# A long convolution and a state-space layer on one core: spectra kept on one partition, output stage in array pieces, queues in a new order

## The chip, the cores and the metric

The kernel runs on one core of a Trainium2 chip. A core has a matrix engine (TensorE, PE in the profile, with PEld for its weight loads), a vector engine (VectorE, DVE), a scalar engine (ScalarE, ACT), GpSimd (POOL) and SyncE (SP); POOL and SP issue nearly all transfers here, and sixteen DMA engines carry them. Each engine works through its own instructions in order. The metric is device time in microseconds; lower is better.

## The reference, cut to what matters

Two layers with S = 2048 positions and D = 1024 channels in bfloat16; their results stand side by side in the output, 2048 x 2048.

```python
# A: short causal convolution, gate, long convolution by FFT, gate
k_shift = sum over t < 4 of k_pad[:, t:t+S, :] * shift_k[:, 3 - t]
kv = k_shift * v
y  = irfft(rfft(kv, 2*S) * rfft(ssm_k, 2*S))[:S]      # along the positions
a  = q * (y + kv * ssm_D)
# B: diagonal complex state space
Bu = x @ B_bar.T                                      # complex, P = 1024 states
h  = Lam_bar * h + Bu[t]        for every position t
b  = 2 * real(hseq @ C.T) + x * Dskip
out = concatenate([a, b])
```

Lam_bar and B_bar come from the small parameters Lambda, log_dt and B.

## The kernel before, in words

All work is cut into some 1240 tasks. Each task is a small function stored under a short name in the table `E`; a hand-written string `ORDER` (lines 66 to 144) lists the tasks one after another. A word such as `sa.1.0:d0` calls `E["sa"](1, 0)` and gives it PSUM buffer `d0`. The letters behind the colon are buffers: `p` single and `d` double accumulator banks in PSUM (two `p`, three `d`), `a`, `b`, `e`, `m`, `w` rings of tiles in SBUF. A suffix `@S` or `@G` puts a transfer on SP's or POOL's queue, `@D` or `@G` puts a copy on the vector engine or GpSimd. Since every engine takes its instructions in program order, the string fixes the order on all of them. Line 168 (`spd`) and line 169 (`gpd`) issue the transfers: SP unless the word says G, POOL unless it says S.

Layer A is a Fourier transform of length 4096 at odd half frequencies, split as 128 x 32, with 16 residues r of the position.

- `kp`, `vp` load k and v; `kvm`, `kva`, `kvb`, `kvc` (lines 575 to 604) form the gated product on the vector engine, two residues at a time, eight chains in all. `am` (610) multiplies by the first-stage matrix `F1t`, `ae` evicts, `ast` stores to the scratch tensor `Ys_kv` in DRAM.
- `hl` loads the filter, `hT` (630) transposes it on PE, `hm` (643) transforms it, `he` evicts, `hst` stores to `Ys_h`.
- The second stage runs over 16 groups gq of frequencies. `lh` and `lk` load a group's 512 KB from the two scratch tensors, `lw` a pair of groups' weights. `sh` and `sk` (668 to 681) transform it with 64x64 pieces of the array, four matmuls a call; `she` and `ske` evict. Real and imaginary part of a spectrum then stand in different blocks of 32 partitions. For the complex product the other part is needed too: `sw` (694) copies each block of 32 partitions of `hab` to its neighbour with four DMAs a group. `pr` (701) multiplies on the vector engine, `sa` (707) does the first half of the inverse with eight 64x64 matmuls a call and two calls a group, `sae` evicts, `vst` stores to `Vs`.
- The output stage: `vl` loads a residue from `Vs`, `a3` (739) multiplies by `Gt`, 128 x 128, half of which is zeros; `a3e` evicts, `qm` multiplies by q (loaded by `qp`), `ost` stores.

Layer B runs over 16 chunks i of 128 positions. `bl`, `bT`, `bc` load, transpose and copy the 16 blocks of B to `BT`; `cx` and `x` (480, 483) bring C and x through transposing DMAs on SP. `U` (486) is the input product, 16 matmuls of 128 columns a call; `ue` evicts; `r1`, `r2`, `sc`, `cm`, `r3`, `r4` (500 to 537) are rotation, scan, carry and rotation back on the vector engine, one chunk after another; `y` (539) is the output product, four matmuls of 512 columns a call, `ye` evicts and `yst` stores. The order string mixes layer B's U and y blocks between the steps of layer A.

The parameters, their tables (`tabA1`, `par_rest`, `eo`, `stt`) and the broadcast of the short filter (`ld_w`, `wb`, `wbe`) stand in the first lines of the string. Tiles of the pool a1 (the ring of k and the broadcast filter) give way to those of a2 once the first stage is done.

Of the kernel before, what the change touches and what calls it, by code (L numbers as in the profile page):

```python
# [27 lines left out]
def a_constants():  # L28
# [4 lines left out]
    G1 = np.zeros((2, 2, 32, 2, 64, 2))  # L33
    for h in range(2):
        F1[:, h, :, h] = np.transpose(F, (0, 2, 1, 3))
        G1[h, :, :, :, :, h] = np.transpose(F, (1, 3, 2, 0)) * (2 / NFFT)
# [5 lines left out]
    WF = np.zeros((2, N2, 2, 32, 3, N2))  # L42
# [3 lines left out]
    WF[:, :, :, :, 2, :] = WF[:, :, :, :, 0, :]  # L46
    WI = np.zeros((2, 2, N2, 16, 2, 2, N2, 2))
    for gi in range(2):
        for ui in range(2):
            for gq in range(16):  # L50
                cc = np.transpose(c_[ui, 2 * gq + gi], (1, 0)); ss = np.transpose(s_[ui, 2 * gq + gi], (1, 0))
                o = WI[gi, :, :, gq, ui]
                o[0, :, 0, :, 0] = cc; o[0, :, 0, :, 1] = ss
                o[1, :, 0, :, 0] = -cc; o[1, :, 0, :, 1] = -ss
                for cp in range(2):
                    o[cp, :, 1, :, 0] = -ss; o[cp, :, 1, :, 1] = cc
    W = np.concatenate([WF.reshape(128, NWP, 4 * 96), WI.reshape(128, NWP, 2 * 256)], axis=2)
# [9 lines left out]
ld_par bl.4.0@G:b0 bl.5.0@G:b1 bl.5.1@G:b2 bl.4.1:b3 bl.6.0:b4 bl.2.1@G:b5 ld_sd@S bl.1.1@G:b6 ld_w@S:a0a1 kp.0@G kp.-2 ld_F par_T:p0 hl.2@G:a2  # L67
bl.7.0:b7 bT.4.0:p1 p32 exp1 bl.6.1:b8 hl.3@G:a3 bc.4.0 dve2 x.0:b9 kp.-1@G bT.5.0:p0 dve3 sm_pre bT.4.1:p1 bc.5.0 hl.1@G:a4 bl.0.1:b10 bc.4.1
bl.7.1@G:b11 x.4:b12 bT.6.0:p0 tabA1:a5a6a7a8 bc.6.0 bl.2.0:b13 hl.0:a9 exp2 bl.0.0:b0 sin0 rt@G kp.1 bT.1.1:p1 x.2:b1 bT.5.1:p0 tabA2 bc.1.1 cx.4.1
wb.7:p1 bc.5.1 par_rest vp.0@G:a10 ld_G@S sin2 wb.4:p0 cx.5.1 wbe.4 sin1 wb.6:p0 cx.0.0 wbe.6@D eo.0 bl.3.1:b3 wb.1:p0 wbe.7@D bl.1.0:b4 wbe.1@D  # L70
wb.2:p1 cx.0.1 eo.1 stt.0 wb.0:p0 cx.7.0 wbe.2 stt.1 eo.3 wb.5:p1 bl.3.0:b6 x.1:b2 wbe.5@D wbe.0 stt.3 wb.3:p1 wbe.3 bT.6.1:p0 cx.1.0 dd bT.2.0:p1
# [75 lines left out]
def full_kernel(ctx, tc, A_q, A_k, A_v, A_shift_k, A_ssm_k, A_ssm_D, B_x, B_Lre, B_Lim, B_Bre, B_Bim,  # L147
# [96 lines left out]
    def k8(name, shape):  # L244
        return rtile(ap_pool("a2"), "e", name, shape)
# [3 lines left out]
    def once(key, make):  # L249
        if key not in st:  # L250
            st[key] = make()
        return st[key]
# [571 lines left out]
```

## Time and profile before

| | us |
|---|---|
| median of 3 runs | 378.71 |
| lowest and highest run | 377.25, 380.74 |
| span of the profiled execution | 378.5 |
| PE busy in it | 346.6 |
| DVE busy in it | 324.6 |
| ACT busy in it | 264.2 |
| POOL busy in it | 81.3 |

The span goes from the first to the last instruction of the profiled execution, which has no other time of its own. A line of the profile names the source line (L492), the engine, the operation, and the tiles as output <- inputs. Busy time is a union over instructions; a matmul's recorded length includes its way through the array, so the spacing of starts says more than the mean length. The sixteen DMA engines moved 100.06 MB, 264 GB/s on average; the SP queue's packets took 54.8% and POOL's 36.8% of their time.

### The profile page before, as it was taken

To read this page: it belongs to the slowest core of one execution; us is meant where nothing else is said; L and a number is where in the kernel's file an instruction comes from. 1 tells how busy PE (TensorE), PEld (TensorE's weight loads), DVE (VectorE), ACT (ScalarE), POOL (GpSimd) and SP (SyncE) were. 2 spreads that over 40 slices of the span, in tenths; PEclk is the share of its full clock that TensorE was granted. 3 is DMA by queue.
4 is the path that set the end of the run, shared out by engine and by line. 5 is a ranking of instruction groups with operands and counts; after the bars stand their busy time and mean duration, and the time that the engine had idled before them with its cause. 6 is when DMAs were issued, how large, how long until landed. Compare 5 with 4: busy or idle time off the path is not lost.

```text
span 378.5 us, 8748 instructions
## 1 busy us (share of the span) xinstructions
PE 346.6 (92%) x3661; PEld 225.6 (60%) x3661; DVE 324.6 (86%) x229; ACT 264.2 (70%) x341; POOL 81.3 (21%) x150
## 2 busy tenths in 40 slices
PE   4548889899899999999999999989999999999995
PEld 3226678785455578855444757367867664467442
DVE  6989599999999997999997797576899999993972
ACT  4978798877778886952785879778869771346433
POOL 7300023022112521214200325330210202211021
PEclk9999999999999999999999999999999999999999
DMA  6999999997578999999999897999989539877995
GB/s 231 317 338 216 265 272 286 296 314 235 200 243 270 247 313 287 281 272 268 190 275 312 258 324 234 220 267 221 284 236 312 175 125 325 306 229 255 350 319 206
DMA packets 67418, 100.06 MB, mean 264 GB/s; under 512 B 38435, under 2 KB 42147, under 8 KB 67380
## 3 DMA queue, kind: packets, MB, share of 16 engines
q1 hardware_dynamic: 54660, 56.32, 54.8%
q0 software_dynamic: 12720, 43.19, 36.8%
q8 instruction: 28, 0.46, 0.5%
q14 instruction: 10, 0.08, 0.1%
HBM read 49.16 MB, written 33.55 MB: 219 GB/s over the span
## 4 chain that ended last, share of the span: by engine, by line
PE 56%; DMA 15%; issue 13%; ACT 7%; SPq 4%; POOL 2%; DVE 1%; POOLq 0%; ACTq 0%; DVEq 0%
PE ps_u L492 22%; PE ps_y L546 16%; PE ps_a L744 4%; DMA wts<-a_c_W 4%; SPq L483 4%; DMA Ys_kv<-ysb 3%; PE ps_a L643 3%; DMA l2k<-Ys_kv 3%; DMA ld<-in_B_B_re_dram 3%; PE ps_a L717 3%; PE ps_a L610 3%; DMA hab<-hab 2%; PE ps_a L676 2%; PE ps_t L630 2%; ACT ysb L615 2%
## 5 line engine op out<-in xcount | busy, mean ns | idle before, releaser
L492 PEld LDWEIGHTS <-BT 128*128 128x128 bf16 x2048 | 119.3, 98 | 22.6 <-issue 11.7
L492 PE MATMUL ps_u<-xT,BT 128*128 128x128 bf16 x2048 | 127.7, 219 | 2.4 <-ACT u L497 1.2
L546 PE MATMUL ps_y<-CT,h 128*128 128x512 bf16 x512 | 127.7, 379 | 0.0
L546 PEld LDWEIGHTS <-h 128*128 128x128 bf16 x512 | 44.6, 98 | 48.0 <-issue 6.1
L523 DVE TENSOR_TENSOR_SCAN h<-rtab,h 128x2080 bf16<-128x2080 f32 x16 | 71.8, 4488 | 0.2
L497 ACT CAST u<-ps_u 128x512 bf16<-128x512 f32 x64 | 38.2, 603 | 27.0 <-PE ps_u L492 19.1
L506 DVE TENSOR_TENSOR mt<-u,Z 128x4096 bf16<-128x4096 bf16 x16 | 36.7, 2291 | 15.8 <-ACT u L497 15.4
L704 DVE TENSOR_TENSOR hab<-x,hab 128x4096 bf16<-128x4096 bf16 x16 | 36.5, 2286 | 15.2 <-DMA hab<-hab 10.5
L556 ACT CAST yo<-ps_y 128x512 bf16<-128x512 f32 x32 | 19.1, 596 | 28.0 <-PE ps_y L546 24.4
L650 ACT CAST ysbh<-ps_a 128x1024 bf16<-128x1024 f32 x32 | 32.3, 1033 | 8.8 <-PE ps_a L643 7.5
L691 ACT CAST x<-ps_a 128x1024 bf16<-128x1024 f32 x32 | 31.9, 1026 | 8.8 <-PE ps_a L676 5.9
L506 DVE TENSOR_TENSOR mt<-h,Z 128x4096 bf16<-128x4096 bf16 x16 | 36.7, 2292 | 0.5
L724 ACT CAST vsb<-ps_a 128x1024 bf16<-128x1024 f32 x32 | 31.7, 1027 | 6.5 <-PE ps_a L717 6.0
L583 DVE TENSOR_TENSOR mt<-kring,wbc 128x2048 bf16<-128x2048 bf16 (+3 forms) x14 | 35.8, 2592 | 0.4 <-ACT wbc L473 0.2
L615 ACT CAST ysb<-ps_a 128x1024 bf16<-128x1024 f32 x32 | 32.3, 1043 | 2.7 <-issue 1.6
L685 ACT CAST hab<-ps_a 128x1024 bf16<-128x1024 f32 x32 | 32.2, 1030 | 2.1 <-PE ps_a L676 1.9
L551 PE MATMUL ps_y<-Dd,xT 128*128 128x128 bf16 x128 | 28.0, 219 | 0.0
L749 ACT CAST ot<-ps_a 128x1024 bf16<-128x1024 f32 x16 | 15.7, 1018 | 14.1 <-PE ps_a L744 14.1
L169 POOL DMA_DIRECT2D Ys_h<-ysbh x20 | 14.3, 716 | 43.3 <-ACT ysbh L650 43.3
L168 POOL DMA_DIRECT2D hab<-hab x32 | 15.6, 494 | 32.1 <-ACT hab L685 18.3
L458 PE MATMUL ps_t<-ident,ld 128*128 128x128 bf16 x128 | 13.9, 285 | 9.1 <-DMA ld<-in_B_B_re_dram 4.4
L643 PE MATMUL ps_a<-hT,F1t 128*128 128x512 bf16 x64 | 20.6, 402 | 0.8 <-ACT ysbh L650 0.6
(116 smaller groups left out, 381.8 us busy)
## 6 DMA issues: line engine op xcount, KB each, us to landing
Ys_h<-ysbh POOLq DMA_DIRECT2D x20, 256.0 KB, 5.5
l2h<-Ys_h SPq DMA_DIRECT2D x9, 512.0 KB, 9.7
Vs<-vsb SPq DMA_DIRECT2D x9, 512.0 KB, 4.3
vv<-Vs SPq DMA_DIRECT2D x9, 512.0 KB, 5.2
Ys_kv<-ysb POOLq DMA_DIRECT2D x17, 256.0 KB, 6.2
l2k<-Ys_kv SPq DMA_DIRECT2D x8, 512.0 KB, 3.9
hab<-hab SPq DMA_DIRECT2D x32, 128.0 KB, 5.4
l2k<-Ys_kv POOLq DMA_DIRECT2D x8, 512.0 KB, 7.8
```

Source lines behind the costliest of these rows:

```text
L492: nc.tensor.matmul(pu[:, w, jl, :], BT[:, 2 * jp + jl, w, d, :], xT[:, d, :], start=(d == 0), stop=(d == ND - 1))
L497: nc.scalar.copy(u[:, :, 2 * jp:2 * jp + 2, :], st["pu", i, jp][:])
L506: nc.vector.tensor_mul(m, s_, w_)
L523: nc.vector.tensor_tensor_scan(gf, rtab[:].rearrange("p a j t -> p (a j t)"), gf, 0.0, ALU.mult, ALU.add)
L546: nc.tensor.matmul(py[:], h[:, 1 - w, j, 2:TP], CT[:, j, w, dh * 512:(dh + 1) * 512], start=(j == 0 and w == 0), stop=(j == NJ - 1 and w = ...
L583: nc.vector.tensor_mul(m[:, :, j0:j0 + n, :], a_, wbc[:, j0:j0 + n, :].unsqueeze(1).to_broadcast([P, 2, n, DV]))
L615: nc.scalar.copy(st["ysb", r, u][:], st["pa", r, u][:].rearrange("p e d -> p (e d)"))
L643: nc.tensor.matmul(pd[:, e, :], F1t[:, u, :], st["hT", f, rp][:, e, :], start=True, stop=not sk)
L650: nc.scalar.copy(st["yh", f, rp, u][:], st["pa", f, rp, u][:])
L685: nc.scalar.copy(hab[:, a, :, e * 512:(e + 1) * 512], st["ps", key, gq, e][:])
L691: nc.scalar.copy(x16[:, :, e * 512:(e + 1) * 512], st["ps", "k", gq, e][:])
L704: nc.vector.tensor_mul(hab, x16.unsqueeze(1).to_broadcast([P, 2, 2 * D]), hab)
```

## The change

The matrices and tasks of the second and third stage of layer A, and the order string as a whole.

- `sh` and `sk` now compute only the real or only the imaginary part of a group in a call (argument `c_`), for both halves of the channels, with eight matmuls of 64 rows and 32 columns of the array. Real and imaginary part of one frequency thus land on the same partition, side by side in the free dimension. The weights lose the repeated block.
- `sw` and its 64 DMAs are gone. `pr` writes all four products of a real or imaginary part with another to a tile of its own: still 4096 elements a partition.
- `sa` is one call a group with 32 matmuls of 32 rows and 64 columns of the array. It sums the four products with three weight blocks (the weights of a group pair grow from 896 to 1024 columns) and takes two double banks at once.
- `vl` loads two residues of one half u. `a3` uses 64x64 pieces without the zeros of the old matrix, eight matmuls a call, two calls for each of eight pairs of residues. `qm` works on a pair at once. `qp` and `ost` move 64 partitions, 256 KB, each.
- The vector engine's working tile (`mt`) moves from the common ring to the pools a1 and a2; `hab`'s pool has two buffers instead of three, and four more `a` buffers come in a2. The raw parameters lie in unused rows of `ones`. `kp` of the shifted start loads three slots in one task instead of four in two.
- The order string is written anew for every engine and queue. Of its start: eleven of the sixteen B loads are on POOL (six before), three transposing loads stand ahead of the first `U` (fourteen before), the filter's transposes and `hm` come earlier, and the broadcast filter's copies are all on ACT, while eight `bc` copies are on the vector engine (two before). Before the output stage it has `vst.14@G vl.0.1@S:a6 r1.13:m0 r2.13 y.11.0.1 y.10.0.2 vl.0.0@S:a0 a3.0.0:d0 a3.0.1:d2`.

```diff
-    def s2(key, nm, gq, e, o):
+    def s2(key, nm, gq, c_):
         wt = st["w", gq // 2]
         pd = dtile("ps_a")
...
+        for e in range(2):
+            for gi in range(2):
+                for u in range(2):
+                    up = slice(64 * u, 64 * u + 64)
+                    x = 32 * (2 * (u ^ gi) + e)
+                    b0 = ((2 * gq + gi) % 4) * 64 + 32 * c_
+                    nc.tensor.matmul(pd[x:x + 32, u, :], wt[up, b0:b0 + 32],
+                                     st[nm, gq][up, gi, e * 512:(e + 1) * 512], start=True, stop=True,
+                                     tile_position=(64 * u, x))
...
+    def s2e(key, nm, gq, c_):
+        t_ = once((nm, gq), lambda: k4(nm, [P, 2, D]))
+        nc.scalar.copy(t_[:, c_, :], st["ps", key, gq, c_][:].rearrange("p e d -> p (e d)"))
...
-    def sw(gq):
-        hab = st["hab", gq]
-        for b in range(4):
-            o = b ^ 1
-            spd(hab[32 * b:32 * b + 32, 1, :, :], hab[32 * o:32 * o + 32, 0, :, :])
...
     def pr(gq):
-        hab = st["hab", gq][:].rearrange("p a u d -> p a (u d)")
-        x16 = st["x16", gq][:].rearrange("p u d -> p (u d)")
-        nc.vector.tensor_mul(hab, x16.unsqueeze(1).to_broadcast([P, 2, 2 * D]), hab)
+        st["m2", gq] = rtile(ap_pool("a2"), "e", "hab", [P, 2, 2, D])
+        nc.vector.tensor_mul(st["m2", gq][:], st["x16", gq][:].unsqueeze(2).to_broadcast([P, 2, 2, D]),
+                             st["h16", gq][:].unsqueeze(1).to_broadcast([P, 2, 2, D]))
...
-    def sa(gq, e):
...
+    def sa(gq):
+        wt, m = st["w", gq // 2], st["m2", gq]
+        pd = [dtile("ps_a") for _ in range(2)]
+        st["ps", "v", gq] = pd
+        for n_, (a, b, wi) in enumerate(((0, 0, 0), (1, 1, 1), (0, 1, 2), (1, 0, 2))):
+            for e in range(2):
+                for s in range(2):
+                    for u in range(2):
+                        x = 32 * (2 * s + e)
+                        b0 = 4 * 64 + (gq % 2) * 384 + (3 * u + wi) * 64
+                        nc.tensor.matmul(pd[s][64 * u:64 * u + 64, e, :], wt[x:x + 32, b0:b0 + 64],
+                                         m[x:x + 32, a, b, u * 512:(u + 1) * 512], start=(n_ == 0), stop=(n_ == 3),
+                                         tile_position=(x, 64 * u))
...
-    def a3_(r):
...
+    def a3_(r, dh):
+        pd = dtile("ps_a")
+        st["po", r, dh] = pd
+        for u in range(2):
+            for e in range(2):
+                for h in range(2):
+                    ep, hp = slice(64 * e, 64 * e + 64), slice(64 * h, 64 * h + 64)
+                    nc.tensor.matmul(pd[hp, e, :], Gt[ep, u, :], st["vv", r, u][ep, h, dh * 512:(dh + 1) * 512],
+                                     start=(u == 0), stop=(u == 1), tile_position=(64 * e, 64 * h))
...
+    E["ost"] = lambda r, h: gpd(oar[h, r], st["ot", r][64 * h:64 * h + 64, :, :])
```

294 lines of the change are left out of this document (134 added, 160 removed).

## The prediction

> **What bounds the kernel now.** I read the page's busy shares and slices first, then the time chain, then busy times by stage, then the groups by line.
>
> ```profile
> span 378.5 us, 8748 instructions
> ...
> PE 346.6 (92%) x3661; PEld 225.6 (60%) x3661; DVE 324.6 (86%) x229; ACT 264.2 (70%) x341; POOL 81.3 (21%) x150
> ...
> PE   4548889899899999999999999989999999999995
> ```
>
> PE (the matrix engine) is at eight tenths or more from the fifth slice to the last but one, so the question is how much of that is dense work. The chain gives the pace where PE itself is the chain; its columns are start, length, what.
>
> ```profile
> 6.99 4.90 SPq L483
> ...
> 12.71 8.41 SPq L483
> 21.17 5.62 DMA ld<-in_B_B_re_dram
> ...
> 44.11 1.05 PE ps_u L492 x16
> ...
> 127.35 0.86 PE ps_y L546 x4
> ...
> 142.52 0.86 PE ps_a L610 x4
> ...
> 204.53 0.89 PE ps_u L492 x16
> ...
> 224.74 0.56 PE ps_a L717 x8
> ...
> 227.16 0.99 PE ps_a L717 x16
> ...
> 361.12 1.73 PE ps_a L744 x8
> ...
> 374.69 0.58 ACT yo L556
> ```
>
> Sixteen 128-column matmuls take 0.89 us (56 ns each), four 512-column ones 0.86 (216 ns). In the 64x64 array pieces eight more matmuls cost 0.99 - 0.56 = 0.43 us, 54 ns each: a quarter of 216, so four pieces do run at once. The output stage (L744) runs full size, 1.73 / 8 = 216 ns.
>
> ```profile
> 0.00:50.00 50.00, 31.17 (x243) 21.18 (x244) 40.28 (x74) 37.24 (x60) 11.82 (x27) 1.00 1.02 276
> 50.00:100.00 50.00, 46.80 (x590) 36.71 (x588) 48.81 (x25) 39.48 (x50) 11.62 (x19) 1.00 1.03 280
> 100.00:155.00 55.00, 53.70 (x547) 36.57 (x546) 51.55 (x29) 43.75 (x55) 13.84 (x22) 1.00 0.87 262
> 155.00:200.00 45.00, 43.95 (x412) 24.42 (x409) 43.67 (x24) 28.54 (x36) 10.37 (x20) 1.00 1.04 251
> 200.00:310.00 110.00, 106.28 (x1437) 71.73 (x1436) 89.37 (x45) 88.88 (x110) 23.13 (x45) 1.00 0.87 248
> 310.00:371.00 61.00, 61.00 (x431) 33.54 (x429) 49.76 (x36) 24.90 (x33) 9.43 (x15) 1.00 0.87 297
> ```
>
> These rows are stages: length, then busy PE, PEld, DVE, ACT, POOL, then granted clock, DMA share, GB/s. To 50 us loads bound (DMA 1.02, PE 31 of 50). From 50 to 200 DVE (the vector engine) is busy 144.0 of 150 us and paces the rest. From 200 PE is the bound, and from 310 to 371 it never idles: work taken off PE there comes off the time in full.
>
> **The change, part by part.** The sum is made against this execution's span, 378.5 us; the median of the runs shown is 378.71, 0.2 above.
>
> *Output stage in pieces: -6.9.* Old a3: 16 calls of 4 full matmuls, 64 x 216 ns = 13.8 us. New: 16 calls of 8 matmuls in 64x64 pieces, 128 x 54 ns = 6.9. All lie after 310 us, on PE.
>
> *Spectra in pieces of 64x32 and 32x64: 0.* sh and sk have 256 matmuls at 54 ns now (13.8 us) and get 512; sa has 256 (13.8) and gets 512. In each case the matmul fills half the area, and eight pieces fit where four did. Eight at once are 216 / 8 = 27 ns each and leave 13.8 and 13.8. The nearest rows show no matmul spaced closer than 54 ns on average; at that pace they cost 27.6 and 27.6, +27.6 in all. I take 27, because the four-piece group already loses nothing, and because the pieces write separate accumulator banks by row group, as now; 54 is the slow rival's price.
>
> [...]
>
> *Changes of array shape: +2.6.*
>
> ```profile
> 206.78 1.06 PE L492 MATMUL ps_u<-xT,BT 128*128 128x128 bf16 x16
> 207.77 1.06 PE L717 MATMUL ps_a<-hab,wts 64*64 64x512 bf16 x16
> 208.66 0.39 PE L676 MATMUL ps_a<-l2h,wts 64*64 64x512 bf16 x4
> 208.98 4.19 PE L492 MATMUL ps_u<-xT,BT 128*128 128x128 bf16 x72
> ```
>
> In this timeline of PE the 16 matmuls before a visit need 0.89 of the 0.99 us, and the five groups of four inside need 5 x 0.216 = 1.08 of the 1.21 us: 0.23 us for going into pieces and back. Counted in the two order strings, PE makes 39 such visits now and 48 in the new order (28 + 13 + 7 by shape, with 5 direct changes between shapes at about 0.1): 9 x 0.23 + 0.5 = 2.6.
>
> *DVE ahead of PE: -2.7.* The rows of DVE by line:
>
> ```profile
> L523 DVE TENSOR_TENSOR_SCAN h<-rtab,h 128x2080 bf16<-128x2080 f32 x16 | 71.8, 4488 | 0.2
> ...
> L506 DVE TENSOR_TENSOR mt<-u,Z 128x4096 bf16<-128x4096 bf16 x16 | 36.7, 2291 | 15.8 <-ACT u L497 15.4
> L704 DVE TENSOR_TENSOR hab<-x,hab 128x4096 bf16<-128x4096 bf16 x16 | 36.5, 2286 | 15.2 <-DMA hab<-hab 10.5 <-ACT x L691 4.6
> ...
> L535 DVE TENSOR_TENSOR h<-mt 128x2048 bf16<-128x2048 bf16 x16 | 19.6, 1223 | 0.5
> ...
> L597 DVE TENSOR_TENSOR mt<-mt 128x4096 bf16<-128x4096 bf16 x8 | 18.3, 2285 | 0.1
> L717 PE MATMUL ps_a<-hab,wts 64*64 64x512 bf16 x256 | 18.2, 383 | 0.8 <-DVE hab L704 0.7
> L583 DVE TENSOR_TENSOR mt<-kring,wbc 128x8192 bf16<-128x8192 bf16 x4 | 17.7, 4424 | 0.3 <-ACT wbc L473 0.2
> ...
> L676 PE MATMUL ps_a<-l2h,wts 64*64 64x512 bf16 x128 | 11.3, 387 | 3.0 <-DMA wts<-a_c_W 2.3 <-DMA l2h<-Ys_h 0.7
> ```
>
> One kv chain (kvm, kva, kvb, kvc) is 4.4 + 2.3 + 1.2 + 1.2 = 9.2 us; one recurrence step (r1, r2, sc, cm, r3, r4) 2.3 + 1.2 + 4.5 + 0.3 + 2.3 + 1.2 = 11.8; a product pr 2.3. Both engines work in order, so for each PE instruction that needs a DVE result I set the DVE work queued up to that result against the PE work queued ahead of the instruction; the largest difference is idle that the order forces on PE. Now it is at y.6.1: eight kv chains, seven steps, two products and about 22 us of tables and copies (DVE's 40.28 busy up to 50 us less the two kv chains in it), 183, against 152 of PE work (64 U at 0.89, 48 y at 0.92, 64 hm and am at 0.43, the rest 23): 31.6 before rounding. In the new order it is at sa.4: 200.5 (eight kv chains, eight steps less two r3 and r4, seven products) against 171.6, 28.9. The product keeps its 4096 elements a partition and a broadcast operand like L506's, so its 2.3 stays. Bounds: 0, if the steps of PE before y.6.1 still wait as now, and -5.4 for twice this.
>
> *Start: -3.0.* The chain's head shows SP held by two x transposes, 4.90 and 8.41 us, with B loads queued behind them; the load that PE wants comes out at 21.17 and lands 5.62 later. Fourteen transposes stand ahead of the first U in the order string, three in the new one (cx.7.0, x.0, cx.2.0), and 11 instead of 6 B loads go by POOL. PE gets h transposes and h matmuls first. What this can give is the idle of the pacing DVE, 50 - 40.28 = 9.7 us in the first stage. DMA is at 1.02 there, so bytes still set the pace: bounds 0 and -9.7; I take a third, since the eleven transposes are only moved to the next stages, where DMA stands at 1.03 and 0.87 and eight BT copies come to DVE instead of two.
>
> [...]
>
> *Exchange removed: -2.0.* 64 DMAs of 128 KB go, 8.4 MB of SBUF traffic, and with them the product's wait.
>
> ```profile
> Vs<-vsb POOLq DMA_DIRECT2D x7, 512.0 KB, 4.5
> vv<-Vs POOLq DMA_DIRECT2D x7, 512.0 KB, 5.2
> ...
> hab<-hab SPq DMA_DIRECT2D x32, 128.0 KB, 5.4
> ...
> hab<-hab POOLq DMA_DIRECT2D x32, 128.0 KB, 7.0
> ```
>
> Of the 10.5 us that L704 waited for them, PE felt L717's 0.7; L676 lost 3.0 to weights and spectra that shared the DMA engines. Bounds 0 and -3.8; I take half, as the weights are still two buffers deep, and eight loads of them grow from 224 to 256 KB.
>
> *New wait ahead of the output: +2.5.* vl reads what all sixteen vst wrote. In the new order, from sae.14.0 (the last eviction) to a3.0.0, PE has six U blocks at 0.89 and five y blocks at 0.92, about 10 us, of which ACT needs 2 to evict. The way is POOL issue 0.5, vst 4.5, vl 5.2: 10.2 to 10.6 against 8. vst.14 also sits behind yst.8 and qp.0.1 on POOL. Now the cover is 14 y blocks, 13 us. Bounds 0 (if PE is late there anyway) and +5 for a second load that queues.
>
> *Without weight.* q and output in halves of 64 partitions: as many bytes, in the tail, where DMA is at 0.87; if that cover went, one 256 KB transfer, about 5 us. Parameters in a corner of ones, one shift load fewer, one qm per pair (-1.2 us of DVE, after its wait): off the path. ACT loses six BT copies and gains four wbc copies and rt, in the start, where it is at 37.24 of 50 us. The working tile that moves from the ring into the two staged pools opens its second life at cm.3, after the last kv chain.
>
> Sum: 378.5 - 6.9 + 2.6 - 2.7 - 3.0 - 2.0 + 2.5 = **369.0**.
>
> **The rivals.**
> 1. *The start opens wide.* Loads first, DVE loses its whole 9.7 us of idle, PE all 3.8 of waiting in the spectra, and the output wait is hidden: 378.5 - 6.9 + 2.6 - 2.7 - 9.7 - 3.8 = 358. For it: SP's held 13.3 us. Against: DMA at 1.02.
> 2. *The order gains nothing.* The transposes come back as waits in the next stage, only PE's own terms stay: 378.5 - 6.9 + 2.6 + 2.5 = 376.7. For it: DMA at 1.03 from 50 to 100 us.
> 3. *Eight pieces do not run at once* (slower). At 54 ns both spectra stages pay: 369.0 + 27.6 = 396.6; if one of the two shapes does it, 382.8. It decides from 27 + 9.5 us / 1024 = 36 ns a matmul on. For it: no row under 54. Against: four pieces scale exactly.
> 4. *Accumulators.* sa now takes two of three double banks at once, and PE may wait for an eviction of 1.03 us before each: 16 x 1.03 = 16.5, 385.5. Against: U and y, on other banks, stand between in most places of the new order.
>
> ```profile
> L724 ACT CAST vsb<-ps_a 128x1024 bf16<-128x1024 f32 x32 | 31.7, 1027 | 6.5 <-PE ps_a L717 6.0
> ```
>
> **How the numbers follow.** Forecast 0.54, rival 1 0.19, rival 2 0.12, rival 3 0.10, rival 4 0.05. Predicted is the forecast's 369.0. One per cent, about what a measurement of this kernel can tell from no change, is 3.8 us. Faster takes rival 1 and all but 0.03 of the forecast: 0.70. Same takes rival 2 and that 0.03: 0.15. Slower takes rivals 3 and 4: 0.15. The range runs from 356, a little under rival 1, to 384, over the cheaper half of rival 3, and leaves out most of rivals 3 and 4 and a tail of rival 1, under 0.2.
>
> **What would show it.** A group of eight piece matmuls should take 0.22 us in a PE timeline, not 0.43; the L744 stage's matmuls should sum to about 7 us; PE busy from 310 us on as now. The first U should start before 40 us instead of 44.1. Idle at L676 by weights should fall under 2 us, and a gap of some 2 us should stand ahead of a3.0.0. Wrong would be: DVE idle over 10 us to 50 us, PE waiting on ACT before sa, or matmuls of 64x32 and 32x64 at 50 ns.

## The result and the profile after

The changed kernel is slower. Its median is 394.82 us (5 runs, 389.60 to 403.38), that of the kernel before 380.74 us (5 runs beside it); the ratio is 1.040 with a 95% interval of 1.030 to 1.051. A second measurement gave 1.044 (1.021 to 1.067). Ratios leave out runs more than 1.5% above the fastest of the same kernel beside them, so they are not exactly quotients of medians. The profiled execution is the run of 389.60 us, the fastest of the five, with a span of 387.8, 9.3 us more than the 378.5 before; the medians are 14.1 us apart. The prediction was 369.0, between 356 and 384.

The page of the changed kernel first: engine totals, then PE in 40 slices and its granted clock.

```profile
span 387.8 us, 9691 instructions
...
PE 337.6 (87%) x4179; PEld 220.5 (57%) x4237; DVE 323.2 (83%) x223; ACT 263.0 (68%) x341; POOL 75.1 (19%) x136
...
PE   3585778898899997939999897999999999999994
...
PEclk9998899999999999987999999999999999999999
```

PE is busy for 9.0 us less than before (346.6 to 337.6) in a longer span, so it waits more. The 3 in the eighteenth slice is a hole that the kernel before does not have. The same stages as in the prediction, in the same columns:

```profile
0.00:50.00 50.00, 30.34 (x242) 20.70 (x246) 37.11 (x72) 37.95 (x57) 12.68 (x28) 0.93 0.88 267
50.00:100.00 50.00, 42.81 (x578) 35.81 (x588) 45.16 (x26) 44.24 (x61) 15.71 (x27) 1.00 1.00 275
100.00:155.00 55.00, 50.11 (x533) 34.99 (x540) 50.29 (x28) 35.86 (x46) 14.47 (x24) 1.00 0.92 261
155.00:200.00 45.00, 37.92 (x505) 21.86 (x511) 33.58 (x19) 28.62 (x35) 6.39 (x12) 0.92 0.76 214
200.00:310.00 110.00, 105.47 (x1599) 63.83 (x1619) 101.38 (x51) 83.66 (x102) 12.81 (x24) 1.00 0.62 190
310.00:371.00 61.00, 59.76 (x666) 38.34 (x672) 50.42 (x28) 26.43 (x37) 11.30 (x18) 1.00 0.83 263
```

DVE, the pacing engine from 50 to 200 us before with 144.0 of 150 us, is down to 129.0 there, and PE with it. From 155 to 200 us PE does 37.9 us of work instead of 44.0.

The array pieces did what the forecast said. In PE's timeline a row is start, length, operation, piece size, shape and count:

```profile
182.91 1.07 PE L713 MATMUL ps_a<-hab,wts 32*64 32x512 bf16 x32
183.91 0.41 PE L685 MATMUL ps_a<-l2k,wts 64*32 64x512 bf16 x8
...
330.80 1.06 PE L742 MATMUL ps_a<-vv,Gt 64*64 64x512 bf16 x16 [0.60 <-DMA vv<-Vs]
```

Recorded lengths overlap: in the kernel before, a matmul of 512 columns has a mean length of 379 ns (L546) and a spacing of 216, so about 0.16 us at the end of a row is length beyond the spacing. Without it, 32 inverse matmuls take 0.91 us, 8 spectrum matmuls 0.25, 16 output matmuls 0.90; in experiment 1 below, 16 spectrum matmuls take 0.63 us and 8 take 0.41, so eight more cost 0.22. In these rows a group of eight 64x32 or 32x64 pieces, and of four 64x64 pieces, takes 0.22 to 0.25 us, about the 216 ns of one full matmul.

**An account of PE.** Busy time does not add up to the span, so I counted PE's time from the starts of its matmuls. Each matmul is given its time at full rate (216 ns for 512 columns, 56 for 128, a quarter or an eighth of that in pieces): their sum is the work, which is thus a count at these rates and the same in every kernel with the same matmuls. Between two matmuls of different array shape up to 0.125 us of the spacing is booked as a shape change. All other spacing is idle (a matmul at a lower clock shows there too), by the time at which it ends. What lies behind the last matmul is the tail. Matmuls whose records are missing (up to 58) are put in from the order string. In us:

| kernel | work | shape | idle to 50 | 50 to 155 | 155 to 200 | 200 to 310 | from 310 | tail | span |
|---|---|---|---|---|---|---|---|---|---|
| before | 318.0 | 7.9 | 33.0 | 8.3 | 1.8 | 5.6 | 0.0 | 4.0 | 378.5 |
| changed | 311.1 | 10.5 | 31.1 | 15.1 | 9.1 | 4.2 | 1.0 | 5.8 | 387.8 |
| changed, second profile | 311.1 | 10.5 | 33.7 | 15.0 | 7.2 | 4.4 | 1.1 | 5.8 | 388.7 |

After less before: work -6.9, shape +2.6, idle -1.9, +6.8, +7.3, -1.4 and +1.0, tail +1.8: +9.3. The arithmetic brought what was forecast for it; 14 us of new idle between 50 and 200 us took that and more. The account closes for these two profiles; it does not cover the further 5 us by which the medians differ. The chain of waits shows the larger single piece:

```profile
161.16 6.98 DMA Ys_kv<-ysb
...
169.03 4.30 DMA l2k<-Ys_kv
...
173.38 1.05 PE ps_a L685 x10
```

This is the turn through DRAM between the two stages of the convolution: the last result of `am` is stored to Ys_kv, lands 7 us later, only then is the first load issued, and PE has the first `sk` as its next instruction (idle 6.3 us; the account has 6.5). DVE loses 9.8 us here, because its next instruction is the product that needs this `sk`. The other piece, between 50 and 155 us, is in the waits of that stretch (engine, its line, what it waited for, us in total, times, longest), first of the changed kernel, then of the kernel before:

```profile
ACT ysbh L657 <- DMA Ys_h<-ysbh: 6.7, 3, 4.2
ACT ysb L622 <- DMA Ys_kv<-ysb: 5.8, 3, 3.3
...
PE ps_a L617 <- ACT ysb L622: 3.7, 4, 2.1
...
PE ps_t L637 <- ACT hT L642: 1.7, 1, 1.7
...
PE ps_a L650 <- ACT ysbh L657: 1.5, 1, 1.5
```

```profile
ACT hT L635 <- DMA Ys_kv<-ysb: 2.0, 1, 2.0
```

Before, ACT waited 2.0 us in this stretch for a store to leave a staging tile, now 12.5; PE then waits for ACT's evictions. That the first makes the second is a reading of these rows, not yet a test of it.

### The profile page after: what moved, and what is told of

Its sections match the earlier page's. It is cut to its first block, busy times and chain, and to the rows that moved or that the text cites. A ratio compares the mean times of both kernels' runs of the same rounds, so it can differ in the third digit from the quotient of the medians.

```text
span 387.8 us, 9691 instructions
## 1 busy us (share of the span) xinstructions
PE 337.6 (87%) x4179; PEld 220.5 (57%) x4237; DVE 323.2 (83%) x223; ACT 263.0 (68%) x341; POOL 75.1 (19%) x136
## 4 chain that ended last, share of the span: by engine, by line
PE 37%; issue 14%; DMA 12%; ACT 4%; DVE 4%; POOL 2%; SPq 1%; POOLq 0%; another core or an unknown queue 0%; ACTq 0%; DVEq 0%
PE ps_y L552 16%; PE ps_u L498 12%; PE ps_a L685 3%; DMA Ys_kv<-ysb 3%; PE ps_a L713 3%; DMA l2k<-Ys_kv 2%; ACT ysb L622 2%; DVE mt L512 2%; DMA Vs<-vsb 2%; DMA vv<-Vs 1%; DMA l2h<-Ys_h 1%; DVE h L529 1%; DMA xT<-in_B_x_dram 1%; PE ps_y L557 1%; ACT u L503 1%
## 5 line engine op out<-in xcount | busy, mean ns | idle before, releaser
L498 PE MATMUL ps_u<-xT,BT 128*128 128x128 bf16 x2048 | 129.0, 220 | 1.1 <-DMA xT<-in_B_x_dram 0.4
L552 PE MATMUL ps_y<-CT,h 128*128 128x512 bf16 x475 | 123.1, 384 | 3.2 <-DMA CT<-in_B_C_im_dram 1.1
L552 PEld LDWEIGHTS <-h 128*128 128x128 bf16 x512 | 44.8, 99 | 52.1 <-issue 13.1
L699 DVE TENSOR_TENSOR hab<-x,h 128x4096 bf16<-128x4096 bf16 x16 | 36.6, 2289 | 18.7 <-ACT x L693 16.4
L503 ACT CAST u<-ps_u 128x512 bf16<-128x512 f32 x64 | 38.3, 602 | 14.1 <-PE ps_u L498 12.8
L693 ACT CAST x<-ps_a 128x1024 bf16<-128x1024 f32 x32 | 32.1, 1020 | 12.6 <-PE ps_a L685 12.5
L657 ACT CAST ysbh<-ps_a 128x1024 bf16<-128x1024 f32 x32 | 32.9, 1040 | 11.4 <-DMA Ys_h<-ysbh 7.2
L693 ACT CAST h<-ps_a 128x1024 bf16<-128x1024 f32 x32 | 31.6, 1021 | 6.6 <-PE ps_a L685 4.3
L173 POOL DMA_DIRECT2D Ys_h<-ysbh x23 | 16.7, 725 | 50.2 <-ACT ysbh L657 50.1
L464 PE MATMUL ps_t<-ident,ld 128*128 128x128 bf16 x128 | 11.7, 252 | 11.3 <-DMA ld<-in_B_B_re_dram 6.4
L650 PE MATMUL ps_a<-hT,F1t 128*128 128x512 bf16 x54 | 19.1, 417 | 2.7 <-ACT ysbh L657 1.5
L748 ACT CAST ot<-ps_a 128x1024 bf16<-128x1024 f32 x16 | 15.7, 1020 | 7.7 <-PE ps_a L742 7.7
L752 DVE TENSOR_TENSOR ot<-ot,qt 128x2048 bf16<-128x2048 bf16 x8 | 9.7, 1222 | 12.7 <-ACT ot L748 10.7
```

Source lines behind the costliest of these rows:

```text
L498: nc.tensor.matmul(pu[:, w, jl, :], BT[:, 2 * jp + jl, w, d, :], xT[:, d, :], start=(d == 0), stop=(d == ND - 1))
L503: nc.scalar.copy(u[:, :, 2 * jp:2 * jp + 2, :], st["pu", i, jp][:])
L552: nc.tensor.matmul(py[:], h[:, 1 - w, j, 2:TP], CT[:, j, w, dh * 512:(dh + 1) * 512], start=(j == 0 and w == 0), stop=(j == NJ - 1 and w = ...
L657: nc.scalar.copy(st["yh", f, rp, u][:], st["pa", f, rp, u][:])
L693: nc.scalar.copy(t_[:, c_, :], st["ps", key, gq, c_][:].rearrange("p e d -> p (e d)"))
L699: nc.vector.tensor_mul(st["m2", gq][:], st["x16", gq][:].unsqueeze(2).to_broadcast([P, 2, 2, D]), st["h16", gq][:].unsqueeze(1).to_broadca ...
```

## The experiments

My theory was that the new order loses time in these two places, by too little PE work ahead of the first `sk` and by staging slots reused right behind their stores, while the new arithmetic gains. The rival was that the arithmetic itself loses, or that the waits only move when they are mended. The account of every kernel, in the columns of the table above:

| kernel | work | shape | idle to 50 | 50 to 155 | 155 to 200 | 200 to 310 | from 310 | tail | span |
|---|---|---|---|---|---|---|---|---|---|
| 1 work ahead of sk | 311.1 | 9.8 | 33.8 | 17.1 | 12.8 | 6.9 | 0.8 | 5.8 | 398.1 |
| 2 slots | 311.1 | 10.4 | 34.0 | 20.5 | 8.2 | 4.3 | 0.7 | 5.8 | 395.0 |
| 3 both | 311.1 | 10.0 | 34.5 | 19.2 | 12.6 | 5.6 | 0.9 | 5.8 | 399.6 |
| 4 stores early | 311.1 | 10.9 | 32.8 | 19.0 | 11.4 | 2.8 | 1.4 | 5.8 | 395.0 |
| 5 old, late kv | 318.0 | 8.0 | 32.1 | 10.0 | 1.8 | 2.7 | 0.0 | 4.2 | 376.7 |
| 6 two loads later | 311.1 | 10.7 | 32.8 | 17.4 | 6.4 | 4.2 | 1.0 | 5.8 | 389.4 |
| 7 ACT relief | 311.1 | 10.6 | 32.0 | 13.4 | 6.8 | 5.0 | 1.2 | 5.8 | 386.0 |
| 8 new, mended | 311.1 | 10.6 | 32.3 | 15.3 | 3.9 | 5.6 | 0.3 | 5.8 | 384.8 |
| 9 old order | 311.1 | 13.2 | 31.2 | 7.3 | 0.7 | 6.1 | 6.4 | 5.0 | 380.9 |
| 9 its tail mended | 311.1 | 13.1 | 29.7 | 15.7 | 2.2 | 5.4 | 3.3 | 5.6 | 386.1 |
| 9 in pairs | 311.1 | 11.8 | 31.3 | 11.8 | 0.6 | 4.7 | 2.5 | 8.3 | 381.8 |
| 9 pairs, early end | 311.1 | 12.1 | 28.7 | 13.7 | 1.3 | 5.4 | 7.2 | 3.8 | 383.3 |
| 10 old front, new rest | 311.1 | 10.5 | 32.7 | 19.9 | 9.6 | 3.0 | 4.0 | 5.3 | 396.0 |
| 10 new front, old rest | 311.1 | 13.2 | 32.3 | 22.1 | 4.7 | 9.4 | 4.6 | 5.2 | 402.5 |
| 11 old, no exchange | 318.0 | 8.0 | 32.1 | 9.1 | 0.9 | 1.3 | 0.0 | 4.3 | 373.5 |

Stages are cut by the clock, so a kernel that is late shifts some idle to the next column. Each row is one profile, and the kernels ran on several chips, each beside the kernel before.

**1. More PE work ahead of the first `sk`.**

```diff
-... sh.2.1:d2 sk.0.0:d1 ...
+... sh.2.1:d2 y.3.1.1 y.3.0.3 ye.3.0:b0 y.3.1.2 U.6.3.0:p0 y.3.1.3 r3.2:m0 r4.2 U.6.3.1 ue.6.3
+ye.3.1 y.2.0.0:p0 y.2.1.0:p1 y.2.0.1 y.2.1.1 sk.0.0:d1 ...
```

> The changed kernel with fifteen words of the order (eight y parts, the last U block of chunk 6, its evictions, r3.2 and r4.2) moved ahead of the first kv spectrum sk.0.0, so that PE's own work between the last forward matmul and sk.0.0 grows from about 10.5 to about 20 us. Nothing else changes. My theory (the turn through Ys_kv, store 7.0 and load 4.3 us, is not covered): the 6.3 us stall ahead of sk.0.0 falls under 1 us, DVE's 9.8 us hole ahead of the first product shrinks, and the time falls by about 7 us against the changed kernel: 1.04 times the kernel before becomes 1.02. Rival (the waits are only displaced: PE has to wait for DVE or for loads soon afterwards): the stall goes, but the time stays within 2 us of the changed kernel, 1.035 to 1.045.

Measured: 1.062 (1.043 to 1.081). In its timeline of PE the 6.3 us wait is gone, and this stands behind it:

```profile
185.36 0.41 PE L685 MATMUL ps_a<-l2h,wts 64*32 64x512 bf16 x8 [1.83 <-ACT x L693]
187.44 0.63 PE L685 MATMUL ps_a<-l2k,wts 64*32 64x512 bf16 x16 [1.67 <-DMA l2k<-Ys_kv]
...
189.20 1.92 PE L713 MATMUL ps_a<-hab,wts 32*64 32x512 bf16 x30 [0.80 <-ACT x L693]
...
192.82 0.63 PE L685 MATMUL ps_a<-l2k,wts 64*32 64x512 bf16 x8 [1.14 <-ACT x L693]
```

The moved words had kept the spectra apart; without them PE asks for accumulators that ACT has not yet evicted. The rival's mechanism held: the wait was displaced. The time is more than the rival's 1.045, and one reason lies outside the edit: the idle ahead of 155 us, where nothing was changed, was 4.7 us more than in the first profile of the changed kernel and 2.2 more than in the second.

**2 and 3. Staging slots handed out anew, alone and with the first edit.** Each word of the b ring takes the slot whose last use stands farthest back in the order string (for example `ae.1.1`, `he.1.4.1` and `ae.12.0` leave slots that had just been stored from).

> The changed kernel with the 14 slots of the b ring (staging of the forward results, x, h transposes, y results) handed out anew: each word takes the slot that was free for longest, so that fewer evictions wait for a store that has just been issued from their slot. Order and queues stay as they are. My theory (evictions on ACT wait for stores, 7.2 us at the h staging and 5.8 us at the kv staging, and PE then waits for accumulators): those two waits fall below half, and the time falls by 3 to 6 us, to 1.025 to 1.033 times the kernel before. Rival (from 50 to 155 us the DMA engines at 1.00 and 0.92 set the pace, so that a slot only moves the wait): within 1.5 us of the changed kernel, 1.036 to 1.044.

> Both edits together: the fifteen words ahead of the first kv spectrum and the b slots handed out anew. My theory: the two losses lie in different stages and add, 10 to 13 us less than the changed kernel, 1.005 to 1.015 times the kernel before. Rival (only displaced): no more than the better of the two alone.

Measured: 1.053 (1.027 to 1.078) and 1.069 (1.054 to 1.083). The two edits together are no better than either alone. With the slots alone, PE idles from 50 to 155 us for 5.4 us more than in the changed kernel, and ACT's waits for stores there fall from 12.5 to 10.0 us, not below half. Timeline of PE of experiment 2:

```profile
43.99 1.89 PE L464 MATMUL ps_t<-ident,ld 128*128 128x128 bf16 x16 [6.58 <-DMA ld<-in_B_B_re_dram]
...
56.31 1.03 PE L464 MATMUL ps_t<-ident,ld 128*128 128x128 bf16 x8 [3.21 <-DMA ld<-in_B_B_im_dram]
```

PE waits for B loads: a load had been given a slot that came free late (POOL held it back to 45.33 us; in the changed kernel the last was issued at 36.68). Farthest back in the string is not longest free in time. The test of the slots is inconclusive.

**4. The last kv results leave earlier.** Evictions `ae.13.0` and `ae.15.1` move up, nine stores move up towards their evictions, four slots are changed, `r3.2 r4.2` go ahead of `pr.0` and two y parts ahead of `sk.0.0`.

```diff
-... ae.13.1:b0 cm.2 sc.3 ... ae.3.1:b2 ue.6.1:a0 U.6.2.1 ae.15.1:b1 ... ae.13.0:b4 ...
+... ae.13.1:b2 ae.13.0:b11 ast.13.1@S ast.13.0@G cm.2 sc.3 ... ae.3.1:b0 ast.3.1@S ae.15.1:b1 ast.15.1@S ue.6.1:a0 ...
```

> The changed kernel with the last results of the kv transform leaving earlier: ae.13.0 right behind ae.13.1, ae.15.1 ahead of ue.6.1, seven stores right behind their evictions instead of behind later ones on POOL and SP, three slots of the b ring swapped so that none waits for a store just issued, r3.2 and r4.2 ahead of the first product on DVE, and two y parts of 1.9 us ahead of sk.0.0; what follows sk.0.0 stays. The last store should be issued at about 157 instead of 162 us. My theory (the turn from the last kv store to the first kv load costs the new order 7 us): PE's idle from 155 to 200 us falls from 9.1 (second profile: 7.2) to 3 or less and what stands behind it moves up, so that PE's idle in all (60.5 and 61.4) falls by 5 to 6 us. Rival (displaced, as in the run with fifteen words moved): the stall goes, but the idle comes back at the evictions and loads of the next stage, and the sum from 155 to 310 us stays at 12 to 13.

Measured: 1.051 (1.044 to 1.057). `sk.0.0` no longer waits, but now a load of the h spectrum does, that the edit had put behind the earlier stores on SP's queue:

```profile
172.87 1.27 PE L685 MATMUL ps_a<-l2h,wts 64*32 64x512 bf16 x24 [3.28 <-DMA l2h<-Ys_h]
```

Displaced again; the 11.4 us from 155 to 200 us are no less than before the edit. And its idle from 50 to 155 us is 4 us above the changed kernel's, in words that are nearly all the same.

**5. The reverse in the old kernel: its last kv results 9 us later.**

```diff
-... ae.12.1 ... am.14.0:d2 ae.14.0:b3 ast.14.0 am.14.1:d2 ae.14.1:b4 ast.14.1 ... lk.1@G lk.3 lk.0@G y.4.1.0 ye.3.1 y.4.0.0 lk.2@G ...
+... y.4.1.0 ye.3.1 y.4.0.0 am.14.0:d0 ae.14.0:b3 ast.14.0 am.14.1:d1 ae.14.1:b4 ast.14.1 lk.1@G lk.3 lk.0@G lk.2@G ...
```

> The reverse on the kernel before: its last two kv matmuls am.14.0 and am.14.1, their evictions and stores, and the four loads that follow, are moved about 9 us later on PE (behind y.3.1 and two y parts), all else as it was, so that the cover ahead of the first kv spectrum shrinks from 16 to about 8 us. My theory (cover shorter than store and load, about 11 to 16 us, stalls PE): an idle of 5 to 8 us ahead of sk.3.0, where there is none now, and the time grows by as much, 1.013 to 1.02 times the kernel before. Rival (some other work gives way, or the loads wait for DMA anyway): no idle over 2 us and the time within 0.5 per cent.

Measured: 1.005 (0.998 to 1.012). The first `sk` now follows 8.5 us after the last `am`, 17.1 in the kernel before, and PE's longest wait from 150 to 200 us is 0.7 us. So a short cover alone does not stall PE; my theory falls in this form. POOL's timeline of this kernel, of the changed kernel and of the kernel before tell what differs:

```profile
172.56 0.54 POOL L169 DMA_DIRECT2D Ys_kv<-ysb  x1 [0.38 <-ACT ysb L615]
175.72 1.59 POOL L168 DMA_DIRECT2D l2k<-Ys_kv  x3 [2.62 <-PE ps_y L546]
```

```profile
161.16 1.07 POOL L173 DMA_DIRECT2D Ys_kv<-ysb  x2 [3.92 <-ACT ysb L622]
169.03 1.07 POOL L172 DMA_DIRECT2D l2k<-Ys_kv  x2 [6.80 <-DMA Ys_kv<-ysb]
```

```profile
163.39 0.54 POOL L169 DMA_DIRECT2D Ys_kv<-ysb  x1 [3.21 <-ACT ysb L615]
...
170.51 1.58 POOL L168 DMA_DIRECT2D l2k<-Ys_kv  x3 [5.82 <-DMA Ys_kv<-ysb]
```

In the first of the three, the last two stores go out alone, 0.9 us apart, and each lands 2.3 us after its issue; the load behind them is issued 2.6 us after, and what it waited for last is a y matmul, not the store. In the changed kernel two stores go out together, right behind others on both queues, and land 7.0 us after their issue (5.6 in its second profile); the load has to wait 6.8 us. A late store alone does not stall PE either: in the kernel before, the last one lands 6.2 us after its issue and POOL's loads wait 5.8 us for it. But there PE has 17.1 us of other work from the last `am` to the first `sk`; in the changed kernel it has 12.1 (18.3 less the wait). It takes a late store and a short cover together.

**6. Two other transfers taken out from among the last stores.**

```diff
-... lh.7@G:a6 U.7.1.1 ... she.3.0 x.11:b9 y.3.0.2 ... lk.3@G:a5 ... lk.1@S:a13 ...
+... U.7.1.1 ... she.3.0 y.3.0.2 ... lk.3@G:a5 lh.7@G:a6 ... lk.1@S:a13 x.11:b9 ...
```

> The changed kernel with two transfers moved back that stand among its last kv stores and are needed 40 us later or more: the transpose of x chunk 11 behind lk.1 on SP, the load lh.7 behind lk.3 on POOL. Nothing else changes. My theory (the last stores land 7 us after their issue because they share the DMA engines with these): the last store lands in 4 to 5 us, the idle ahead of sk.0.0 (6.5, second profile 5.1) falls to 3 to 4, and the time by 1.5 to 3 us, 1.03 to 1.035 times the kernel before. Rival (the stores' own bunch, 1.3 MB in 5 us, sets their landing): idle ahead of sk.0.0 within 1 us of 5 to 6.5.

Measured: 1.024 (1.019 to 1.030), 391.39 us. POOL's wait for the last store and PE's for the load:

```profile
170.21 1.07 POOL L172 DMA_DIRECT2D l2k<-Ys_kv  x2 [4.04 <-DMA Ys_kv<-ysb]
```

```profile
174.17 1.06 PE L685 MATMUL ps_a<-l2k,wts 64*32 64x512 bf16 x16 [3.13 <-DMA l2k<-Ys_kv]
```

POOL waits 4.0 us for the store instead of 6.8 (5.4 in the second profile of the changed kernel), PE 3.1 us for the load instead of 6.3. The last two stores land 3.6 us after their issue instead of 7.0 and 5.6. The theory held: other transfers, needed 40 us later, stretched the turn. In time the gain is less sure: the interval touches that of the changed kernel, which did not run beside it.

**7. Five copies taken off ACT.** `rt` goes back to POOL and `wbe.1`, `.5`, `.6`, `.7` to DVE, as in the kernel before.

> The changed kernel with five copies taken off ACT as in the kernel before: rt on POOL instead of ACT, and wbe.1, wbe.5, wbe.6 and wbe.7 on DVE instead of ACT. My theory (ACT, busy 44 of 50 us from 50 to 100 us and full of evictions, is late with what PE waits for there): PE's idle from 50 to 100 us falls by 2 us or more against the 9.3 and 10.3 of the two profiles of the changed kernel, and the first kvm starts earlier than 21 us. Rival (those waits are for stores that hold slots, so ACT's own work does not count): the idle stays within 1 us of 9.3 to 10.3.

Measured: 1.029 (1.021 to 1.038). The idle from 50 to 100 us alone is 9.2 us, as in the changed kernel (9.3 and 10.3): there the rival held. ACT still waits 12.4 us for stores from 50 to 155 us. The first `kvm` waits 2.9 us for the broadcast filter instead of 6.0, but starts at 22.2 us, not ahead of 21. PE's idle in all is 58.5 instead of 60.5 and 61.4; that is 2 to 3 us less, about what the idle to 50 us of the two profiles of the changed kernel differs by (2.6), so a gain by the copies is not shown.

**8. What gained, put together:** edit 7, edit 6, and of edit 4 `ae.13.0`, the stores and `r3.2 r4.2`, with `lh.2` left ahead of the stores.

> The changed kernel with all the edits that gained something: the five copies off ACT, the two transfers later, the last kv evictions and stores earlier but with lh.2 ahead of them, and r3.2 and r4.2 ahead of the first product. PE's words keep their order. My theory (most of the loss ahead of 200 us lies in these waits): PE's idle in all from 60.5 to 54 or less, and 1.015 to 1.025 times the kernel before. Rival (the waits are displaced to the next eviction or load): idle of 58 or more, 1.03 or more.

Measured: 1.013 (1.004 to 1.021). PE's idle in all is 57.3: less than the rival's 58, more than the 54 of the theory, with a ratio as good as the theory's. From 155 to 200 us it is 3.9 instead of 9.1 and 7.2; from 50 to 155 us, 15.3, nothing was won. In us the gain is less than the ratios say: its span is 3.0 and 3.9 us under the two profiles of the changed kernel, and the kernel before was slower beside it (median 382.89 us) than beside the changed kernel (380.74).

**9. The new arithmetic in the old order**, in four steps: the old words, without `sw`; then the two product slots handed to the output stage too; then the two output calls of a pair next to each other; then the last pair and its stores ahead of the last y parts.

```diff
-... sa.1.0:d0 sa.1.1:d2 sae.1.0:a0 ... pr.0 ... a3.7:d2 ... a3.10:d1 ... qm.11 ... ost.7 ...
+... sa.1:d0d2 sae.1.0:a0 ... pr.0:e1 ... a3.0.0:d2 ... a3.0.1:d1 ... qm.0 ... ost.0.0 ...
```

> The new arithmetic (spectra in 64x32 and 32x64 pieces, no exchange, output stage in 64x64 pieces with halves of q and output) in the OLD order of all queues: the order of the kernel before, without the exchange words, each pair of sa words made one, the k-th of the old output words at the place of the k-th of the new ones, slots of the accumulators and of the 4 KB ring handed out again from the first product on. My theory (the arithmetic gains what was forecast for it, the loss is the new order's): faster than the kernel before, by the 6.9 us of the output stage and up to 2 of the exchange, less about 2 for shape changes: about 372, 0.98 times the kernel before. Rival (the arithmetic itself loses, by sa that takes two of three accumulators, by shape changes, or by the output's pairs that need two loads each): 1.01 or more.

> The new arithmetic in the old order throughout, as before, but with the two product slots, free after the last sa, as two more slots of the output stage and its slots handed out by longest free: in the run before one result tile was given a slot whose store had just been issued, and PE then waited 3.4 us at 352 us. My theory (that wait was of the experiment's making, and the old order hides everything else): the wait goes, 4 us less, 1.005 to 1.01 times the kernel before. Rival (another transfer is late next in the output stage, where pairs need two loads each): 1.02 as before.

> The new arithmetic in the old order, with the two output calls of a pair next to each other, so that PE goes into the 64x64 pieces and back 8 times instead of 14 (6 times 0.21 us less), and the output stage's slots handed out as in the mended run. By PE's account of the kernel before (work 318.0, shape changes 7.9, idle 48.6, 4.0 behind the last matmul) this should give work 311.1, shape 12, idle 45 to 48 (the run without the exchange had 43.5), 5.5 behind the last matmul: 374 to 377, 0.985 to 0.995 times the kernel before. My theory (the parts of the arithmetic are worth what was forecast; the loss is the order's): that. Rival (the old order cannot hide the pairs of loads or the spectra's accumulators): idle of 52 or more, 1.005 or more.

> The new arithmetic in the old order with pairs of output calls, as in the run before it, with the last output pair, its product with q and its stores moved ahead of the last eight y parts: there the span ended 8.3 us behind the last matmul, in the kernel before 4.0. My theory (in the old order the new arithmetic is worth its sum, 6.9 less for 3.9 of shape changes, once its own tail is covered): the end falls to 4 to 5.5 us behind the last matmul and the time to 0.995 to 1.002 times the kernel before. Rival (the end moves into PE's idle): 1.005 or more, with idle over 50 us.

Measured: 1.021 (1.000 to 1.042), 1.026 (1.000 to 1.053), 1.007 (1.001 to 1.013) and 1.014 (1.007 to 1.020). The theory's figures, 0.98 to 1.01, were missed each time, though the first two intervals reach down to 1.000. The 1.007 of the third rests on four of twelve runs, 377.29 to 380.14 us; the median of all twelve is 383.31 us, 1.012 times the 378.63 of the kernel before, and its profile is of a run of 383.58. From 155 to 200 us there is no new idle in any of the four, so that loss is the order's; but the 6.9 us of saved work do not show in the time. In the first step 5.3 us go into shape changes (13.2 against 7.9: the old order has its output calls at 14 places) and 7.4 into idle from 310 us and the tail. With pairs side by side it is 3.9 and 6.8. Moving the end up gave the tail back (3.8) and put this in its place:

```profile
367.18 1.13 PE L742 MATMUL ps_a<-vv,Gt 64*64 64x512 bf16 x12 [2.13 <-DMA vv<-Vs]
```

The new output stage needs two 512 KB loads for the first of two calls and holds both to the second, in a string that was laid out for one load a call.

The four have the same words up to the first spectra, but for one slot, and nearly those of the kernel before. Yet PE idles there from 50 to 155 us for 7.3, 15.7, 11.8 and 13.7 us, the kernel before for 8.3. ACT's waits for stores in this stretch, of the first kernel and of the second:

```profile
ACT hT L640 <- DMA Ys_kv<-ysb: 1.9, 1, 1.9
```

```profile
ACT ysb L622 <- DMA Ys_kv<-ysb: 7.3, 2, 6.5
ACT hT L642 <- DMA Ys_kv<-ysb: 3.3, 2, 1.8
ACT ysbh L657 <- DMA Ys_h<-ysbh: 0.6, 1, 0.6
```

So with one and the same order these waits came to 1.9, 11.2, 7.5 and 7.4 us, and the idle is largest and smallest where they are. Part of the second kernel's idle is a lower clock: 0.95 was granted in the stretch, 1.00 in the first and third, 0.98 in the fourth. At full clock the same order thus gave 7.3 and 11.8 us, and how much of the changed kernel's 15 us, also at full clock, is the new order's cannot be told from this.

**10. Mixed orders,** with the changed kernel on the same chip: old order ahead of the first spectrum and new behind it, and the other way round.

> The new arithmetic with a mixed order: all words that stand ahead of the first spectrum sh.0.0 in the new order (start, forward transforms, first U and y) are done in the old order, all later ones in the new order; slots are kept where they are free and handed out again where not. Theory A (the loss sits in the start and the forward stage, where PE waits for B loads and for staging that DMA and ACT bring late): about 1.00 times the kernel before. Theory B (it sits in the spectra, from the first sk on, where the turn through Ys_kv and the closely set sk, pr and sa leave PE waiting): 1.03 to 1.04, as the changed kernel.

> The other mix: the words ahead of the first spectrum in the old order are done in the new order, all later ones in the old order (its output stage with the two product slots as two more slots for loads and results). Theory A (loss in start and forward stage): 1.03 or more times the kernel before. Theory B (loss in the spectra): 1.00 to 1.01. If both mixes lie near 1.02, the loss is shared.

> The changed kernel itself, on the same chip as the mixed orders, so that they can be read against it. Expected 1.04 times the kernel before by both theories; where its profile is slower than 390 us, the first theory (loads at the start) expects the difference ahead of 100 us, the second (spectra) expects it after 160 us.

Measured: 1.053 (1.016 to 1.090) and 1.081 (1.065 to 1.098), against 1.044 (1.021 to 1.067) for the changed kernel. The second mix is slower than either order, the first cannot be told from the changed kernel. Both idle about 20 us from 50 to 155 us; why is not shown. They are no clean exchange: the first has fewer y and U parts ahead of the first spectrum than the old order, since these stand later in the new one. They do not tell where the loss sits. The repetition shows how far one kernel's front moves: the idle to 50 us is 2.6 us more than in its first profile.

**11. The kernel before without the exchange.**

```diff
-... sw.1 ... sw.0@G ...
+...
```

> The kernel before without the exchange: the 64 transfers of 128 KB between partitions are left out, and the product takes the same half of the spectrum twice, in two instructions, so the kernel leaves out the other half of the complex product. All else is the kernel before. The forecast's step says 2.0 us less (0 to 3.8): weights and spectra land earlier, PE's 3.0 us of idle ahead of the spectra matmuls and 0.7 ahead of the products shrink by half. Rival (these loads wait for free slots or for their stores, not for the DMA engines): PE's idle from 155 to 310 us stays at 7 to 8 us and the time within 1 us.

Measured: 0.996 (0.991 to 1.000). DMA share and PE from 155 us on, to be read against the rows of the kernel before:

```profile
155.00:200.00 45.00, 44.08 (x413) 24.74 (x420) 44.06 (x27) 28.49 (x36) 6.42 (x12) 1.00 0.80 225
200.00:310.00 110.00, 108.70 (x1466) 74.67 (x1478) 95.06 (x60) 91.00 (x113) 11.74 (x22) 1.00 0.57 194
```

DMA falls from 1.04 and 0.87 to 0.80 and 0.57, and PE's idle from 155 to 310 us from 7.4 to 2.2. The exchange is worth about 0.4% by the runs, 1.6 us, and up to 5 by one pair of profiles: the forecast's 2.0 lies in it, and so does, by the runs, next to nothing.

## Why the prediction was wrong, point by point

- *Output stage in pieces, -6.9; spectra in pieces, 0; shape changes, +2.6.* All three right: eight pieces take 0.22 to 0.25 us in the timeline, about one full matmul's 216 ns, the work counted at that rate is 311.1 against 318.0, and shape changes are 10.5 against 7.9.
- *Exchange removed, -2.0.* About right in the old order, 0 to 3.4 us by the runs. In the new order the weights' wait did shrink as said (0.2 us at L685, 2.3 before), and nothing of it reached the span.
- *New wait ahead of the output, +2.5.* Too large: PE waited 0.6 us there. The tail is 1.8 us longer, which the prediction left without weight; that the two together are near 2.5 is luck.
- *Start, -3.0.* Wrong. The first U came at 43.70 us, 0.4 earlier and not before 40, and at 46.94 in the second profile. DVE idled for 12.9 us to 50 us, more than the 10 that the prediction named as a sign of being wrong. The idle to 50 us was 1.9 less in one profile and 0.7 more in the other, one on either side of 0: a gain by the new start is not shown.
- *DVE ahead of PE, -2.7.* This is the step that failed. It took the largest excess of DVE's work over PE's ahead of one PE instruction, 31.6 against 28.9 us, as PE's idle under an order. (The parts that the prediction names for the new order, with the same 22 us of tables and copies, add up to some 199 us, not 200.5; with them the excess is 27.4 and the term -4.2, further off still.) That number is only a lower bound: PE's idle was 48.6 us before and is 60.5 now. What stands above the bound are waits on other engines and on DMA, and for these the new order was never gone through. Two were missed. The turn through Ys_kv, 6.3 us ahead of the first `sk` (4.9 in the second profile): the prediction set the same sum, issue and landing and load against PE's cover, for the output stage and not here. The order made it: the old order has no such wait with either arithmetic, as it covers a store that lands nearly as late, after 6.2 us, by 17.1 us of other work, not 12.1; and in the new order taking two other transfers out from among the last stores brought it down to 3.1. And from 50 to 155 us 6.8 us, where ACT waits 12.5 us for stores that still read its staging tiles, 2.0 before. The prediction costed both at nothing. How much of the 6.8 is the order's is open: the old order with the new arithmetic lost between nothing and 7.4 us there, in part by a lower clock.
- *Rivals.* The price on the slower side was put on pieces that do not run at once, and on accumulators; the first fell, the second shows at no `sa` of the changed kernel. That their 396.6 and 385.5 lie nearest to the measured 394.82 is luck. In mechanism "the order gains nothing" (376.7) was the nearest. That an order can lose 14 us in waits while it moves the same bytes but for the exchange was not among them.

What is shown: the turn's stretch by other transfers, that the loss from 155 to 200 us belongs to the order, and that with the edits of experiment 8 this loss falls from 9.1 and 7.2 to 3.9 us and the ratio from 1.040 to 1.013, of which 3 to 4 us show in the profiles. What is argued only: the slots behind the loss from 50 to 155 us, since the kernel that handed them out anew broke the B loads, and since these waits rise to 11.2 us in the old order too. That part stays open, and so does the rest of the 14.1 us between the medians, which no profile covers. No version tried with the whole computation is faster than the kernel before; the nearest are the new arithmetic in the old order, in pairs, 1.007 by its four fastest runs and 1.012 by all twelve, and the mended new order, 1.013.

## What to carry to other kernels

When an order of queues is replaced, go through each place where one stage's last result becomes the next stage's first operand, above all through DRAM, and set the store's landing among its neighbours plus the load against the work that covers it; either alone says little. The lead that one engine needs over another gives only a lower bound on idle. Before idle in one stretch is put down to an order, profile the same order more than once. Time saved on an engine counts where that engine's next operand is there: here 6.9 us of saved matmul work went into shape changes, a longer tail and waits.

## What the runs showed of the hardware

After the hole ahead of the first `sk` PE did not come back at full rate:

```profile
165.00:170.00 5.00, 2.11 (x18) 0.80 (x16) 1.24 (x1) 1.77 (x2) 0.97 (x2) 1.00 0.35 99
170.00:175.00 5.00, 1.28 (x18) 0.52 (x20) 0.00 (x0) 0.92 (x2) 0.10 (x1) 0.66 0.64 210
175.00:180.00 5.00, 5.00 (x34) 1.84 (x33) 3.96 (x2) 1.96 (x4) 0.53 (x1) 0.66 0.91 219
```

The granted clock (third number from the end) is 0.66 in both later stretches; taken by single microseconds it is 1.00 up to 171 us, 0.80 in the next one, 0.50 from 172 to 178, 0.79 in the next one and 1.00 from 179 on. PE's timeline has the matmuls that ran then:

```profile
175.83 3.39 PE L552 MATMUL ps_y<-CT,h 128*128 128x512 bf16 x9
```

Nine y matmuls take 0.38 us each on average instead of 0.216. The stage's 9.1 us of idle in the account less the 6.5 of the wait leave 2.6, and most of that is this. In this profile the hole was 6.3 us long. Behind the 3.1 us of experiment 6 PE was slow as well: the first y matmul there, at 175.16 us, has a length of 0.61 us. Behind the 1.6 us that were left in experiment 8 it has 0.39 us, and nine y matmuls soon after take 2.11 us, not 3.39. How long a hole has to be for this is not shown.

The last kv stores, 256 KB each, landed 2.3 us after their issue when the two were 0.9 us apart and went out alone, and 3.5 to 7.1 us after it among other transfers (experiments 5 and 6, the changed kernel twice, the kernel before). And the fronts of kernels that share nearly all their words up to 155 us (the changed kernel in its two profiles, and the experiments 1, 4 and 6) differed by 2.5 to 5.6 us of PE idle from the first profile of the changed kernel, as much as the 3 us that the mended turn is worth, or more.
